# An intermediate of a two-stage transform, laid out in DRAM by the first stage's row

## The chip, the cores and the metric

The kernel runs on one core of a Trainium2 chip, in one launch. The metric is the device time of that launch in microseconds. Engines are named as in the profile: PE does matmuls, DVE and POOL element-wise work, ACT activations and copies, SP only issues DMAs (ACT issues some too).

## The reference: what is computed

A causal convolution of length 12480 in two batches of 128 channels, with a filter that a small network makes from position embeddings, and then two dense layers with 2048 hidden units each. Only the convolution is touched by the change.

```
h = (relu(pos_emb @ w1) @ w2) * exp(-0.01 * pos)      # the filter, 12480 x 128
u = x * v                                             # 2 x 12480 x 128
y = causal convolution of u with h along the sequence # in the reference by FFT of length 24960
a = x * y
b = relu(a @ moe_w_in) ** 2 @ moe_w_out
c = b @ moe2_w_in ;  out = (c * cos(c)) @ moe2_w_out
```

## The kernel before

The convolution is a transform by matmuls in two stages (12480 = 104 x 120), a product, and the way back. Stage 1 is a DFT over 104 rows (padded to 112) for each of the 120 columns. Stage 2 is a DFT over the columns for each of the 104 resulting rows, the product of signal and filter spectrum, and the inverse of stage 2. Stage 3 (not touched) does the inverse over 104 and the two dense layers; its inputs come from the intermediate `Ds` in DRAM.

Stage 1 goes in 30 chunks q of two column pairs i. For a chunk, `load` issues four DMAs on SP: positions `pt` (128 rows), `xt`, `vt` and the DFT table `et` (112 rows each), with five buffers each. `mlp1` makes the hidden layer of the filter network, `prep` runs up to five pairs ahead, multiplies x by v on POOL and scales the filter, and `pair` does eight matmuls `A` and the butterfly on ACT, DVE and POOL into `bt` (two buffers, 112 rows x 8 x 384). Each chunk's `bt` is stored to the intermediate `Bs` in DRAM by a DMA on ACT's queue, issued after the first pair of the next chunk. The order of the instructions on each engine is the order of the program. Meanwhile `decode` splits the weights of the dense layers in small steps on DVE, ACT and POOL; each step needs a load of raw weights on SP.

`Bs` is laid out by the second stage's row: [120 rows p, 2 halves c, 112 first-stage rows k, 384]. So a store writes, for each of 112 partitions, eight runs of 384 numbers (1.5 KB), and `load2` of stage 2, which takes four k for all p, reads two runs of 1536 numbers (6 KB) for each of 120 partitions.

Stage 2 goes in 26 groups g of four k. `spectrum` does the matmul `H` of the filter part of a group, `product` the matmuls `Z` of the signal part, `inverse` the way back, `butterfly` writes `dt`, which is stored to `Ds`. B2 has three buffers; `load2(g + 3)` is issued once group g is done with its own.

The end of stage 1 is written by hand. Group 0's B2 lies in a pool of its own, `B20`. With the first pair of the last chunk, SP issues the load of its rows 0 to 111; the rows 112 to 119 come straight from `bt` in SBUF, by `first`: four DMAs of 6 KB for each pair of the last two chunks, 16 in all. The last chunk is stored in two halves by `store1`. Groups 1 and 2 are loaded at the start of stage 2, after the second of these stores.

Of the kernel before, what the change touches and what calls it, by code (L numbers as in the profile page):

```python
# [22 lines left out]
NP = 112  # L23
# [11 lines left out]
WORDER = [0, 1, 2, 3, 4, 5, 6, 7, 8, 12, 9, 13, 10, 14, 11, 15]  # L35
LA = LDB = 5
WRATE = (3, 2, 1, 4)
WS = 54
# [10 lines left out]
def conv_moe(ctx, tc, t):  # L49
# [68 lines left out]

    c0 = ctx.enter_context(tc.tile_pool(name="c0", bufs=1))
    B20 = c0.tile([2 * HB, 2, G4, 384], F32, name="B2_0")  # L120

    def load2(B2, g, rows=slice(0, 2 * HB)):
        nc.sync.dma_start(out=B2[rows].rearrange("p c k e -> p c (k e)"),
                          in_=Bs[rows, :, G4 * g:G4 * (g + 1), :].rearrange("p c k e -> p c (k e)"))


    with ExitStack() as st:
        c1 = st.enter_context(tc.tile_pool(name="c1", bufs=1))
        ld1 = st.enter_context(tc.tile_pool(name="ld1", bufs=LDB))
        io = st.enter_context(tc.tile_pool(name="io1", bufs=2))  # L130
# [8 lines left out]
        ld = {}  # L139
        Bk = Bs.rearrange("p c k e -> k (p c) e")  # L140

        def load(q):
            pt = ld1.tile([128, CB, NP], F32, tag="pos", name="pt")
            xt = ld1.tile([NP, CB, 2, 256], F32, tag="xt", name="xt")
            vt = ld1.tile([NP, CB, 2, 256], F32, tag="vt", name="vt")
            et = ld1.tile([NP, CB, 2, NP], F32, tag="et", name="et")
            nc.sync.dma_start(out=pt, in_=t["posT"][q])
            nc.sync.dma_start(out=xt, in_=t["xl"][q])
            nc.sync.dma_start(out=vt, in_=t["vl"][q])
            nc.sync.dma_start(out=et, in_=t["E"][q])  # L150
            ld[q] = (pt, xt, vt, et)

# [23 lines left out]
        def pair(q, i):  # L176
            if i == 0:
                bt_t[q] = ld1.tile([NP, CB, 2, 2, 384], F32, tag="bt", name="bt", bufs=2)
            et, u, bt = ld[q][3], ut_t[q], bt_t[q]
# [22 lines left out]

        def store1(q, i):
            b = CB * q + i
            nc.scalar.dma_start(out=Bk[:, 4 * b:4 * b + 4, :], in_=bt_t[q][:, i].rearrange("k r c e -> k (r c) e"))

        def first(q, i):
            b = CB * q + i
            for c in range(2):
                for r in range(2):  # L210
                    p = 2 * b + r
                    nc.sync.dma_start(out=B20[p:p + 1, c].rearrange("b k e -> b (k e)"), in_=bt_t[q][0:G4, i, r, c, :])

        def store(q):
            nc.scalar.dma_start(out=Bk[:, 4 * CB * q:4 * CB * (q + 1), :],
                                in_=bt_t.pop(q).rearrange("k b r c e -> k (b r c) e"))

# [18 lines left out]
        for n, (q, i) in enumerate(seq):  # L236
# [5 lines left out]
            if i == 0 and q:  # L242
                store(q - 1)
            if (q, i) == (NCH - 1, 0):
                load2(B20, 0, slice(0, 2 * (HB - 2 * CB)))
            if q >= NCH - 2:
                first(q, i)
            if q == NCH - 1 and i == 1:
                for e in range(CB):
                    store1(q, e)  # L250
            if i == 1:
# [22 lines left out]
    with ExitStack() as st:  # L274
# [6 lines left out]
        decode(WG)  # L281
        NB = 3
        B2 = [B20] + [c2.tile([2 * HB, 2, G4, 384], F32, name=f"B2_{n}") for n in range(1, NB)]

        hs = {}

        def spectrum(g, c):
            H = psH.tile([128, G4, D], F32, tag="H", name="H")
            nc.tensor.matmul(H, Gt[:, c, :], B2[g % NB][:, c, :, 256:384], start=True, stop=True)
            hr = hk.tile([128, G4, D], F32, tag=f"hr{c}", name=f"hr{c}")  # L290
            hi = hk.tile([128, G4, D], F32, tag=f"hi{c}", name=f"hi{c}")
            nc.scalar.activation(hi[0:64], H[64:128], AF.Copy, scale=-1.0)  # L292
            nc.scalar.activation(hi[64:128], H[64:128], AF.Copy)  # L293
            if c == 0:
                for e in range(2):
                    nc.scalar.activation(hr[64 * e:64 * e + 64], H[0:64], AF.Copy)  # L296
            hs[g, c] = (hr, hi, H)
# [10 lines left out]
        def product(g, j, c):  # L308
            hr, hi, _ = hs[g, c]
            Z = psZ.tile([128, 2, 2, D], F32, tag="Z", name="Z")  # L310
            nc.tensor.matmul(Z, Gt[:, c, :], B2[g % NB][:, c, 2 * j:2 * j + 2, 0:256], start=True, stop=True)
            w = wk.tile([128, 2, 2, D], F32, tag="w", name="w")
# [58 lines left out]

        for n in range(1, NB):
            load2(B2[n], n)
        seq = [(g, j) for g in range(NG) for j in range(G4 // 2)]
# [8 lines left out]
        for n in range(len(seq) + 4):  # L383
# [16 lines left out]
            if n < len(seq) and seq[n][1] == 1 and seq[n][0] + NB < NG:  # L400
                load2(B2[seq[n][0] % NB], seq[n][0] + NB)

# [280 lines left out]
def host(inp):  # L683
# [6 lines left out]
    for s, d in (("x", "xl"), ("v", "vl")):  # L690
        a = inp[s].reshape(2, N1, 2, NCH, CB, D)
        out[d] = c(pad(a.transpose(3, 1, 4, 2, 0, 5), 1)).reshape(NCH, NP, CB, 2, 256)
    p = inp["pos_emb"].reshape(N1, 2, NCH, CB, 64)
    out["posT"] = c(pad(p.transpose(2, 1, 4, 3, 0), 4)).reshape(NCH, 128, CB, NP)
    out["w1"] = c(inp["w1"])
# [25 lines left out]
```

## Time and profile before

| | |
|---|---|
| median of three runs | 2890.15 us (2887.17 to 2894.08) |
| the profiled execution's own time | 2895.59 us |
| its span from first to last instruction | 2893.8 us |
| PE, DVE, ACT, POOL busy over the span | 96%, 84%, 86%, 49% |
| DMA moved | 214.99 MB, mean 74 GB/s |

Busy time is the time with an instruction running. An idle time of an engine is put down to what released it last. A DMA is seen twice: as an issue on the queue of an engine (SPq, ACTq), which is short, and as packets on the 16 DMA engines.

### The profile page before, as it was taken

How to read it: one execution, taken by the hardware profiler on the slowest of the kernel's cores; microseconds unless marked ns; L12 is line 12 of the kernel's file. 1: busy time of each engine (PE TensorE's matmuls, PEld its weight loads, DVE VectorE, ACT ScalarE, POOL GpSimd, SP SyncE). 2: the span in 40 equal slices, each digit the busy share in tenths (PEclk: the TensorE clock that was granted, in tenths of full speed). 3: DMA queues.
4: the chain of work that ended last, by engine and by line, in shares of the span. 5: the costliest groups of instructions: out<-in, count | busy, mean ns of one | idle time of the engine just before them, and what ended most of it. 6: DMA issues, size and time to landing. Idle time of an engine off the chain costs nothing.

```text
span 2893.8 us, 39390 instructions
## 1 busy us (share of the span) xinstructions
PE 2770.2 (96%) x11740; PEld 2117.5 (73%) x11740; DVE 2418.6 (84%) x4844; ACT 2488.1 (86%) x4464; POOL 1420.7 (49%) x1112
## 2 busy tenths in 40 slices
PE   6778699889999999999999999999999999999999
PEld 3444233378888888888888888888888888888887
DVE  4778688878888888888888888888888888888888
ACT  4455699869999999999999999999999999999998
POOL 4666578714444444444444444444444444444445
PEclk9889799989999999999999999999999999999999
DMA  9998888721010111101100101111110001010000
GB/s 283 290 303 268 218 256 260 205 77 29 16 33 24 31 28 30 30 27 31 27 31 16 31 27 31 27 31 30 27 30 27 26 21 31 27 31 27 19 8 9
DMA packets 111661, 214.99 MB, mean 74 GB/s; under 512 B 7344, under 2 KB 85224, under 8 KB 111448
## 3 DMA queue, kind: packets, MB, share of 16 engines
q1 hardware_dynamic: 83217, 170.80, 20.6%
q10 hardware_dynamic: 28231, 41.69, 4.3%
q8 instruction: 92, 1.51, 0.2%
q14 instruction: 121, 0.99, 0.1%
HBM read 132.72 MB, written 79.63 MB: 73 GB/s over the span
## 4 chain that ended last, share of the span: by engine, by line
PE 78%; ACT 8%; DMA 2%; issue 2%; DVE 2%; SPq 0%; POOL 0%; POOLq 0%; DVEq 0%; ACTq 0%
PE h L490 13%; PE h L492 12%; PE h L491 12%; PE y L506 12%; PE y L505 12%; PE y L504 12%; PE pc L456 3%; ACT w L314 2%; ACT w L313 2%; ACT hr L296 1%; ACT hi L292 1%; DMA B<-Bs 1%; ACT ds L343 1%; ACT hi L293 1%; PE A L184 1%
## 5 line engine op out<-in xcount | busy, mean ns | idle before, releaser
L595 POOL TENSOR_TENSOR gl<-g,gh 128x512 fp32r<-128x512 f32 (+2 forms) x800 | 1034.1, 1293 | 1258.3 <-ACT gh L586 764.3
L578 DVE TENSOR_TENSOR g<-h,c 128x512 f32<-128x512 f32 (+2 forms) x800 | 537.6, 672 | 246.3 <-ACT c L570 239.8
L490 PE MATMUL h<-zh,wh 128*128 128x512 f32 (+2 forms) x1600 | 643.3, 402 | 0.7 <-DVE zh L474 0.7
L555 ACT ACTIVATE k<-h,quarter 128x512 int32<-128x512 f32 (+2 forms) x800 | 541.0, 676 | 114.6 <-PE h L492 100.5
L506 PE MATMUL y<-gl,wh 128*128 128x512 f32 (+2 forms) x1600 | 625.2, 391 | 5.2 <-POOL gl L595 2.5
L492 PE MATMUL h<-zh,wl 128*128 128x512 f32 (+2 forms) x1600 | 624.1, 390 | 0.0
L504 PE MATMUL y<-gh,wl 128*128 128x512 f32 (+2 forms) x1600 | 623.4, 390 | 0.1
L491 PE MATMUL h<-zl,wh 128*128 128x512 f32 (+2 forms) x1600 | 623.4, 390 | 0.0
L505 PE MATMUL y<-gh,wh 128*128 128x512 f32 (+2 forms) x1600 | 622.7, 389 | 0.0
L570 ACT ACTIVATE c<-r,halfpi 128x512 f32<-128x512 f32 (+2 forms) x800 | 565.2, 706 | 2.6 <-DVE r L563 2.6
L529 ACT ACTIVATE r<-h 128x512 f32<-128x512 f32 (+2 forms) x800 | 471.8, 590 | 99.8 <-PE h L492 83.1
L549 DVE TENSOR_TENSOR gl<-g,gh 128x512 fp32r<-128x512 f32 (+2 forms) x800 | 535.8, 670 | 1.0
L563 DVE CUSTOM_DVE_ANT_0 r<-h,k 128x512 f32<-128x512 f32 (+2 forms) x800 | 534.0, 667 | 0.0
L535 ACT ACTIVATE g<-r 128x512 f32<-128x512 f32 (+2 forms) x800 | 492.5, 616 | 2.1 <-DVE gl L549 1.5
L542 DVE CAST gh<-g 128x512 fp32r<-128x512 f32 (+2 forms) x800 | 331.1, 414 | 41.7 <-ACT g L535 40.0
L506 PEld LDWEIGHTS y<-gl,wh 128*128 128x128 f32 x1600 | 301.8, 189 | 76.8 <-POOL gl L595 7.7
L504 PEld LDWEIGHTS y<-gh,wl 128*128 128x128 f32 x1600 | 302.2, 189 | 67.2 <-DVE zl L517 0.5
L492 PEld LDWEIGHTS h<-zh,wl 128*128 128x128 f32 x1600 | 302.6, 189 | 66.6
L505 PEld LDWEIGHTS y<-gh,wh 128*128 128x128 f32 x1600 | 302.1, 189 | 66.6
L490 PEld LDWEIGHTS h<-zh,wh 128*128 128x128 f32 x1600 | 303.2, 190 | 58.1 <-DVE zh L474 0.9
L491 PEld LDWEIGHTS h<-zl,wh 128*128 128x128 f32 x1600 | 302.9, 189 | 56.1
L586 ACT ACTIVATE gh<-g 128x512 fp32r<-128x512 f32 (+2 forms) x400 | 246.2, 615 | 0.1
(65 smaller groups left out, 2671.9 us busy)
## 6 DMA issues: line engine op xcount, KB each, us to landing
Bs<-bt ACTq DMA_DIRECT2D x29, 1344.0 KB
B<-Bs SPq DMA_DIRECT2D x25, 1440.0 KB
dt<-Ds SPq DMA_DIRECT2D x59, 416.0 KB
Ds<-dt SPq DMA_DIRECT2D x25, 960.0 KB
xt<-xl SPq DMA_DIRECT2D x30, 448.0 KB
vt<-vl SPq DMA_DIRECT2D x30, 448.0 KB
xt<-xT SPq DMA_DIRECT2D x60, 208.0 KB
out<-o SPq DMA_DIRECT2D x47, 256.0 KB
```

The source lines that it names most:

```text
L490: nc.tensor.matmul(h[:, :n], wh[:, f, :], zh[:, :n], start=True, stop=False)
L491: nc.tensor.matmul(h[:, :n], wh[:, f, :], zl[:, :n], start=False, stop=False)
L492: nc.tensor.matmul(h[:, :n], wl[:, f, :], zh[:, :n], start=False, stop=True)
L504: nc.tensor.matmul(y[:, :n], wl[:, f, :], gh[:, :n], start=a, stop=False)
L505: nc.tensor.matmul(y[:, :n], wh[:, f, :], gh[:, :n], start=False, stop=False)
L506: nc.tensor.matmul(y[:, :n], wh[:, f, :], gl[:, :n], start=False, stop=b)
L549: nc.vector.tensor_tensor(out=gl[:, :n], in0=g[:, :n], in1=gh[:, :n].bitcast(F32), op=ALU.subtract)
L555: nc.scalar.activation(k[:, :n], hp[2, u][:, :n], AF.Identity, scale=-1.0, bias=quarter)
L563: nc.vector._custom_dve(TENSOR_ADD_SAT, out=r[:, :n], in0=h[:, :n], in1=k[:, :n], s0=0.25, s1=-0.75)
L570: nc.scalar.activation(c[:, :n], r[:, :n], AF.Sin, bias=halfpi, scale=TWO_PI)
L578: nc.vector.tensor_tensor(out=g[:, :n], in0=h[:, :n], in1=c[:, :n], op=ALU.mult)
L595: nc.gpsimd.tensor_tensor(out=gl[:, :n], in0=g[:, :n], in1=gh[:, :n].bitcast(F32), op=ALU.subtract)
```

## The change

`Bs` becomes [112 k, 240 (p, c), 384]: by the first stage's row. A store now writes one run of 8 x 384 numbers (12 KB) for each of 112 partitions; `load2` reads, for each of 120 partitions, four runs of 768 numbers (3 KB). x, v and the table of a chunk stand side by side in DRAM (`xve`) and come in one DMA of 112 rows x 2496 numbers (10 KB); the positions keep theirs. Both land in one slot of 128 x 3072 numbers. Of the five slots three belong to a pool `ring` that outlives stage 1: they become the three B2 of stage 2. `bt` moves to the pool io.

The hand-written end changes. With the first pair of the last chunk (q = 29), after the store of chunk 28, SP issues `load2` for groups 0, 1 and 2 with rows 0 to 115. After the second pair, ACT's queue stores the first 16 rows (k = 0 to 15) of the last chunk, SP issues `load2` for the three groups with rows 116 to 119, and ACT's queue stores rows 16 to 111. `first`, `store1` and the loads at the start of stage 2 go. Matmuls of stage 2 read B2 with k outside and c inside.

```diff
--- before.py
+++ after.py
@@ -34,6 +34,8 @@
 OFF = 24
 WORDER = [0, 1, 2, 3, 4, 5, 6, 7, 8, 12, 9, 13, 10, 14, 11, 15]
 LA = LDB = 5
+NB = 3
+XVE, SLOT0, SLOT = 2048 + 4 * NP, 2048 + 6 * NP, 3072
 WRATE = (3, 2, 1, 4)
 WS = 54
 WG = 16
@@ -116,17 +118,24 @@
         for _ in range(n):
             next(steps, None)
 
-    c0 = ctx.enter_context(tc.tile_pool(name="c0", bufs=1))
-    B20 = c0.tile([2 * HB, 2, G4, 384], F32, name="B2_0")
-
-    def load2(B2, g, rows=slice(0, 2 * HB)):
-        nc.sync.dma_start(out=B2[rows].rearrange("p c k e -> p c (k e)"),
-                          in_=Bs[rows, :, G4 * g:G4 * (g + 1), :].rearrange("p c k e -> p c (k e)"))
+
+    conv_st = ExitStack()
+    ring = conv_st.enter_context(tc.tile_pool(name="ring", bufs=NB, side="right"))
+    Bg = Bs.rearrange("k (p c) e -> p k (c e)", c=2)
+    B2 = {}
+
+    def slot(name, pool=ring):
+        return pool.tile([128, SLOT], F32, tag="ld", name=name)
+
+    def load2(g, rows=slice(0, 2 * HB)):
+        if g not in B2:
+            B2[g] = slot("B2").rearrange("p (k c e) -> p k c e", k=G4, c=2)
+        nc.sync.dma_start(out=B2[g][rows].rearrange("p k c e -> p k (c e)"), in_=Bg[rows, G4 * g:G4 * (g + 1), :])
 
 
     with ExitStack() as st:
         c1 = st.enter_context(tc.tile_pool(name="c1", bufs=1))
-        ld1 = st.enter_context(tc.tile_pool(name="ld1", bufs=LDB))
+        ring1 = st.enter_context(tc.tile_pool(name="ring1", bufs=LDB - NB, side="right"))
         io = st.enter_context(tc.tile_pool(name="io1", bufs=2))
         wk = st.enter_context(tc.tile_pool(name="wk1", bufs=2))
         psA = st.enter_context(tc.tile_pool(name="psA", bufs=6, space=PSUM))
@@ -137,18 +146,15 @@
         win = c1.tile([NP, NCH, CB, 2], F32, name="win")
         tw = c1.tile([NP, 3], F32, name="tw")
         ld = {}
-        Bk = Bs.rearrange("p c k e -> k (p c) e")
 
         def load(q):
-            pt = ld1.tile([128, CB, NP], F32, tag="pos", name="pt")
-            xt = ld1.tile([NP, CB, 2, 256], F32, tag="xt", name="xt")
-            vt = ld1.tile([NP, CB, 2, 256], F32, tag="vt", name="vt")
-            et = ld1.tile([NP, CB, 2, NP], F32, tag="et", name="et")
-            nc.sync.dma_start(out=pt, in_=t["posT"][q])
-            nc.sync.dma_start(out=xt, in_=t["xl"][q])
-            nc.sync.dma_start(out=vt, in_=t["vl"][q])
-            nc.sync.dma_start(out=et, in_=t["E"][q])
-            ld[q] = (pt, xt, vt, et)
+            sl = slot("ld", ring if q % LDB < NB else ring1)
+            nc.sync.dma_start(out=sl[:, XVE:SLOT0], in_=t["posT"][q])
+            nc.sync.dma_start(out=sl[0:NP, 0:XVE], in_=t["xve"][q])
+            x, v = (sl[0:NP, 1024 * n:1024 * (n + 1)].rearrange("p (i a d) -> p i a d", i=CB, a=2) for n in range(2))
+            et = sl[0:NP, 2048:XVE].rearrange("p (i r k) -> p i r k", i=CB, r=2)
+            pt = sl[:, XVE:SLOT0].rearrange("p (i k) -> p i k", i=CB)
+            ld[q] = (pt, x, v, et)
 
         ut_t, hT_t = {}, {}
 
@@ -175,7 +181,7 @@
 
         def pair(q, i):
             if i == 0:
-                bt_t[q] = ld1.tile([NP, CB, 2, 2, 384], F32, tag="bt", name="bt", bufs=2)
+                bt_t[q] = io.tile([NP, CB, 2, 2, 384], F32, tag="bt", name="bt", bufs=2)
             et, u, bt = ld[q][3], ut_t[q], bt_t[q]
             A = {}
             for a in (1, 0):
@@ -200,20 +206,9 @@
             nc.vector.tensor_tensor(out=bt[:, i, 1, 0, :], in0=A[0, 1], in1=v[1], op=ALU.add)
             nc.gpsimd.tensor_tensor(out=bt[:, i, 1, 1, :], in0=e, in1=v[1], op=ALU.subtract)
 
-        def store1(q, i):
-            b = CB * q + i
-            nc.scalar.dma_start(out=Bk[:, 4 * b:4 * b + 4, :], in_=bt_t[q][:, i].rearrange("k r c e -> k (r c) e"))
-
-        def first(q, i):
-            b = CB * q + i
-            for c in range(2):
-                for r in range(2):
-                    p = 2 * b + r
-                    nc.sync.dma_start(out=B20[p:p + 1, c].rearrange("b k e -> b (k e)"), in_=bt_t[q][0:G4, i, r, c, :])
-
-        def store(q):
-            nc.scalar.dma_start(out=Bk[:, 4 * CB * q:4 * CB * (q + 1), :],
-                                in_=bt_t.pop(q).rearrange("k b r c e -> k (b r c) e"))
+        def store(q, rows=slice(0, NP)):
+            nc.scalar.dma_start(out=Bs[rows, 8 * q:8 * (q + 1), :].rearrange("k x e -> k (x e)"),
+                                in_=bt_t[q][rows].rearrange("k b r c e -> k (b r c e)"))
 
         nc.vector.memset(w1b, 0.0)
         nc.vector.memset(w2b, 0.0)
@@ -241,13 +236,16 @@
             upto("mlp", mlp1, (n + lead) // CB + 2 if n else 1, NCH)
             if i == 0 and q:
                 store(q - 1)
-            if (q, i) == (NCH - 1, 0):
-                load2(B20, 0, slice(0, 2 * (HB - 2 * CB)))
-            if q >= NCH - 2:
-                first(q, i)
-            if q == NCH - 1 and i == 1:
-                for e in range(CB):
-                    store1(q, e)
+            if q == NCH - 1:
+                if i == 0:
+                    for g in range(NB):
+                        load2(g, slice(0, 2 * CB * (NCH - 1)))
+                else:
+
+                    store(q, slice(0, 16))
+                    for g in range(NB):
+                        load2(g, slice(2 * CB * q, 2 * HB))
+                    store(q, slice(16, NP))
             if i == 1:
                 upto("load", load, q + LDB + 1, NCH)
             if 2 < n < WS:
@@ -279,14 +277,12 @@
         psH = st.enter_context(tc.tile_pool(name="psH", bufs=HB_, space=PSUM))
         psD = st.enter_context(tc.tile_pool(name="psD", bufs=DB, space=PSUM))
         decode(WG)
-        NB = 3
-        B2 = [B20] + [c2.tile([2 * HB, 2, G4, 384], F32, name=f"B2_{n}") for n in range(1, NB)]
 
         hs = {}
 
         def spectrum(g, c):
             H = psH.tile([128, G4, D], F32, tag="H", name="H")
-            nc.tensor.matmul(H, Gt[:, c, :], B2[g % NB][:, c, :, 256:384], start=True, stop=True)
+            nc.tensor.matmul(H, Gt[:, c, :], B2[g][0:2 * HB, :, c, 256:384], start=True, stop=True)
             hr = hk.tile([128, G4, D], F32, tag=f"hr{c}", name=f"hr{c}")
             hi = hk.tile([128, G4, D], F32, tag=f"hi{c}", name=f"hi{c}")
             nc.scalar.activation(hi[0:64], H[64:128], AF.Copy, scale=-1.0)
@@ -308,7 +304,7 @@
         def product(g, j, c):
             hr, hi, _ = hs[g, c]
             Z = psZ.tile([128, 2, 2, D], F32, tag="Z", name="Z")
-            nc.tensor.matmul(Z, Gt[:, c, :], B2[g % NB][:, c, 2 * j:2 * j + 2, 0:256], start=True, stop=True)
+            nc.tensor.matmul(Z, Gt[:, c, :], B2[g][0:2 * HB, 2 * j:2 * j + 2, c, 0:256], start=True, stop=True)
             w = wk.tile([128, 2, 2, D], F32, tag="w", name="w")
             nc.scalar.activation(w[0:64], Z[64:128], AF.Copy)
             nc.scalar.activation(w[64:128], Z[0:64], AF.Copy)
@@ -369,8 +365,6 @@
                     load_chunk(0, slice(0, N1 - G4))
                     load_aux(1)
 
-        for n in range(1, NB):
-            load2(B2[n], n)
         seq = [(g, j) for g in range(NG) for j in range(G4 // 2)]
         spectrum(0, 0)
         spectrum(0, 1)
@@ -398,7 +392,9 @@
             if n % 2 == 0:
                 decode(WRATE[2])
             if n < len(seq) and seq[n][1] == 1 and seq[n][0] + NB < NG:
-                load2(B2[seq[n][0] % NB], seq[n][0] + NB)
+                load2(seq[n][0] + NB)
+
+    conv_st.close()
 
 
     ck = ctx.enter_context(tc.tile_pool(name="ck", bufs=2))
@@ -689,9 +685,10 @@
     out["xT"] = c(a.transpose(2, 4, 3, 0, 1)).reshape(N2 // CI, D, CI, UT)
     for s, d in (("x", "xl"), ("v", "vl")):
         a = inp[s].reshape(2, N1, 2, NCH, CB, D)
-        out[d] = c(pad(a.transpose(3, 1, 4, 2, 0, 5), 1)).reshape(NCH, NP, CB, 2, 256)
+        out[d] = c(pad(a.transpose(3, 1, 4, 2, 0, 5), 1)).reshape(NCH, NP, 1024)
+    out["xve"] = np.concatenate([out.pop("xl"), out.pop("vl"), out.pop("E").reshape(NCH, NP, 4 * NP)], 2)
     p = inp["pos_emb"].reshape(N1, 2, NCH, CB, 64)
-    out["posT"] = c(pad(p.transpose(2, 1, 4, 3, 0), 4)).reshape(NCH, 128, CB, NP)
+    out["posT"] = c(pad(p.transpose(2, 1, 4, 3, 0), 4)).reshape(NCH, 128, CB * NP)
     out["w1"] = c(inp["w1"])
     out["w2"] = c(inp["w2"])
     for n in _W:
@@ -710,7 +707,7 @@
     arrays = host(inputs)
     t = {n: nc.dram_tensor(n, a.shape, mybir.dt.from_np(a.dtype), kind="ExternalInput").ap() for n, a in arrays.items()}
     t["out"] = nc.dram_tensor("out", (D, NT), F32, kind="ExternalOutput").ap()
-    t["Bs"] = nc.dram_tensor("Bs", (2 * HB, 2, NP, 384), F32).ap()
+    t["Bs"] = nc.dram_tensor("Bs", (NP, 4 * HB, 384), F32).ap()
     t["Ds"] = nc.dram_tensor("Ds", (2, 2 * HB, N1, 256), F32).ap()
     with tile.TileContext(nc) as tc:
         with tc.manual_schedule():
```

## Rows read from the trace of the kernel before

**Rows 1.** The page of the profiled execution: the span, the busy time of the engines, and three lines of the span cut into 40 equal slices of 72.3 us (busy share of PE and of the DMA engines in tenths, and what the latter moved).

```profile
span 2893.8 us, 39390 instructions
...
PE 2770.2 (96%) x11740; PEld 2117.5 (73%) x11740; DVE 2418.6 (84%) x4844; ACT 2488.1 (86%) x4464; POOL 1420.7 (49%) x1112
...
PE   6778699889999999999999999999999999999999
...
DMA  9998888721010111101100101111110001010000
GB/s 283 290 303 268 218 256 260 205 77 29 16 33 24 31 28 30 30 27 31 27 31 16 31 27 31 27 31 30 27 30 27 26 21 31 27 31 27 19 8 9
```

**Rows 2.** The table by stage: the start and end of each stretch, its length, the busy time of each engine with its instructions, PE's granted clock (as a share of 2.4 GHz), the mean busy share of the 16 DMA engines and what they moved. The stretches are stage 1 while it loads, stage 1 after its last load, the transition before and after the first matmul of stage 2, and stage 2.

```profile
37.70:248.90 211.20, 165.63 (x487) 94.12 (x486) 153.12 (x286) 105.01 (x252) 130.03 (x104) 0.88 0.95 303
248.90:290.80 41.90, 35.48 (x105) 19.46 (x103) 36.50 (x71) 23.05 (x51) 25.29 (x22) 0.91 0.70 227
290.80:304.20 13.40, 0.05 (x1) 0.08 (x1) 5.82 (x12) 1.26 (x2) 5.28 (x4) 0.50 0.77 214
304.20:319.90 15.70, 8.84 (x11) 3.31 (x12) 5.50 (x10) 5.91 (x10) 3.81 (x3) 0.61 0.84 210
319.90:571.00 251.10, 232.74 (x507) 90.94 (x505) 209.14 (x328) 241.88 (x409) 201.58 (x159) 0.99 0.83 239
```

**Rows 3.** The DMA issues of the whole span: destination and source, the queue that issues, how many, and KB each.

```profile
Bs<-bt ACTq DMA_DIRECT2D x29, 1344.0 KB
B<-Bs SPq DMA_DIRECT2D x25, 1440.0 KB
...
Ds<-dt SPq DMA_DIRECT2D x25, 960.0 KB
xt<-xl SPq DMA_DIRECT2D x30, 448.0 KB
vt<-vl SPq DMA_DIRECT2D x30, 448.0 KB
...
et<-E SPq DMA_DIRECT2D x30, 196.0 KB
...
pt<-posT SPq DMA_DIRECT2D x30, 112.0 KB
...
B<-bt SPq DMA_DIRECT2D x16, 6.0 KB
```

**Rows 4.** The waits of the engines in stage 1 while it loads (37.7 to 248.9 us): who waited for whom, us in total, times, longest.

```profile
DVE bt L198 <- DMA Bs<-bt: 27.5, 9, 5.1
```

**Rows 5.** The waits of SP's queue in the whole of stage 1 (0 to 292 us), same columns.

```profile
SPq L150 <- PE A L184: 123.9, 23, 12.2
```

**Rows 6.** The timeline of the transition (268 to 325 us): start, length, engine, line, operation, count, and in brackets the idle time before it and what ended it. SPq and ACTq are the queues that issue DMAs.

```profile
285.56 0.31 ACTq L215 DMA_DIRECT2D Bs<-bt  x1
...
286.87 0.56 DVE L198 TENSOR_TENSOR bt<-A,v 112x384 f32<-112x384 f32 x1 [0.95 <-DMA Bs<-bt]
...
290.25 0.54 DVE L200 TENSOR_TENSOR bt<-A,v 112x384 f32<-112x384 f32 x1
...
292.73 0.65 SPq L123 DMA_DIRECT2D B<-Bs  x1
...
293.48 11.11 SPq L212 DMA_DIRECT2D B<-bt  x8
...
304.15 3.82 PE L289 MATMUL H<-B,Gt 120*128 120x512 f32 x4 [16.21 <-DMA B<-Bs]
...
306.02 18.14 SPq L123 DMA_DIRECT2D B<-Bs  x3
306.23 0.59 ACT L292 ACTIVATE hi<-H 64x512 f32<-64x512 f32 x1 [7.35 <-PE H L289]
...
317.85 2.05 PE L289 MATMUL H<-B,Gt 120*128 120x512 f32 x2 [6.86 <-DMA B<-Bs]
...
319.94 0.59 ACT L292 ACTIVATE hi<-H 64x512 f32<-64x512 f32 x1 [7.65 <-PE H L289]
```

**Rows 7.** The DMA queues (q1 is SP's, q10 ACT's) in eight short windows in which one kind of transfer is all or nearly all there is: packets, MB, and the time that the packets took as a share of 16 engines' time in the window. In order: weights on 128 rows, 306.6 to 308 us (mostly 1 KB runs) and 308 to 309 (mostly 4 KB runs); stage 1's loads, 15 to 20; the first load of B on 112 rows, 298 to 300; a load of B on 120 rows, 312 to 317; stores of Bs, 258 to 261 and 267 to 268.5; the last stores of Ds, 584 to 585.

```profile
q1 hardware_dynamic: 492, 0.51, 103.4%
...
q1 hardware_dynamic: 136, 0.44, 107.5%
...
q1 hardware_dynamic: 560, 1.34, 104.8%
...
q1 hardware_dynamic: 76, 0.45, 106.6%
...
q1 hardware_dynamic: 180, 1.01, 95.1%
...
q10 hardware_dynamic: 596, 0.92, 99.2%
...
q10 hardware_dynamic: 344, 0.52, 101.6%
...
q1 hardware_dynamic: 90, 0.32, 88.4%
```

**Rows 8.** The timeline of SP's queue in stage 2 (345 to 565 us), two loads of B in a row of one group each.

```profile
459.04 0.84 SPq L123 DMA_DIRECT2D B<-Bs  x1
...
468.81 0.84 SPq L123 DMA_DIRECT2D B<-Bs  x1
```

## The prediction

> **What bounds the kernel now.** I read the page first, for its slices [rows 1]: the DMA engines are at 7 to 9 tenths in the first eight slices of 40 and at 2 or less after, while PE is full from slice 10 on. So the change, which touches only the first two stages, has to be priced there; the 2,320 us behind them are bound by PE and only move as a whole. The table by stage [rows 2] says what each part is bound by. Stage 1, while it still loads (37.7 to 248.9 us), holds the DMA engines at 0.95 with DVE at 73% and PE at 78%: it is bound by DMA. After its last load (to 290.8) the share falls to 0.70 and DVE is at 87%. From 290.8 to 319.9 lies the transition: PE works 8.9 us of 29. Then stage 2 runs with ACT busy 241.9 of 251.1 us, and no wait of an engine for a transfer is listed there; its loads follow each other every 9.77 us [rows 8], and that is ACT's time for a group.
>
> The chain in stage 1 runs through the store: DVE waited 27.5 us in nine places for a store to land before it could write a bt buffer again [rows 4], and SP's loads waited 123.9 us for PE to let go of the table [rows 5]. In the transition [rows 6], the last bt is written at 290.8, the big load of group 0 is issued at 292.73 when a store has landed, eight small `first` DMAs take SP until 304.6, H starts at 304.15, and ACT then idles another 7.65 us for group 1, whose load was issued at 306.02.
>
> **Prices of DMA.** From windows in which one kind of transfer is alone [rows 7] I take MB / (us x 16 x share), the rate of one engine while it is busy. Weights on 128 rows: 22.0 GB/s with 1 KB runs, 25.6 GB/s with mostly 4 KB runs. Stage 1's loads on 112 rows: 16.0. The load of B: 13.2 with 112 rows, 13.3 with 120. Stores of 1.5 KB runs: 19.3 and 21.3. Stores of Ds with 4 KB runs: 22.6.
>
> The same rows show how many engines take part. A transfer alone of 112 or 128 rows shows 103 to 108% (packets overlap a little), that of 120 rows 95.1%, that is 15.2 of 16. 112 and 128 split into 16 equal shares, 120 into 15 of 8 rows. My reading: a transfer goes to as many engines, up to 16, as share its rows equally. 116, the rows of the new first loads, is 4 x 29, so four engines would do all of it.
> The Trainium skill has this as a rule (DMA: Bandwidth & Descriptors, section "Why a DMA increments its semaphore by 16 and not by 1"): the largest number up to 16 that divides the outermost counts of both sides. By that rule 112 rows go to 16, 120 to 15, 116 and 4 rows to 4; the trace agrees for 112 and 120, and no row here shows four. It speaks against the change, and the sum below is the same with or without it.
>
> **The change, part by part.**
> *Store.* A chunk's store is 1344 KB [rows 3], 1.376 MB, now in 112 runs of 12 KB in place of 896 of 1.5 KB. At 20.3 GB/s (middle of the two rows) it costs 4.24 us of all 16 engines; at the 22.6 of the 4 KB runs 3.81, at the best rate of any row (25.6) 3.36. No row of a store gets slower with longer runs. So -0.43 us a chunk, between 0 and -0.88.
> *Loads.* The same 1204 KB a chunk [rows 3] in two DMAs, x, v and table as one run of 10 KB. SP's issue time is hidden behind its wait for PE, so it is worth nothing. The rate stays that of 112 rows, 16.0; if long runs on 112 rows bring it to the 13.2 of the 6 KB runs, a chunk's 1.233 MB cost 5.84 us in place of 4.82, +1.0. I take nothing, as the row nearest in place and in rows is this stage's own.
> *Shared slots.* x and v were free once POOL had multiplied them, the table once PE was done; now the whole slot waits for PE. SP issues in order and already stood at the table's load, so pt, x and v of the next chunk move back by up to one chunk of 9.6 us. They then have about two chunks until POOL needs them, against a load of 4.8 us beside a store of 4.2. Nothing, unless loads get slower, in which case PE and POOL wait next.
> Stage 1 together: 23 chunks x 0.43 x 0.95 = -9 us; bounds -20 and +23.
> *Transition.* The 16 `first` DMAs go, and with them SP's 11.11 us [rows 6]. In their place three loads of 116 rows, 1392 KB each by 120 rows' 1440 [rows 3], 4.28 MB in all, are issued where the old one was, at 292.7 (the store before must have landed, as now). On four engines that is 1.07 MB each. The slow rates of 13 to 16 belong to loads that run on 15 or 16 engines at once, some 200 to 260 GB/s in all; four engines ask for 100. So I take 24, inside the 22.0 to 25.6 of the undisturbed loads: 44.5 us. Bounds: 41.8 at 25.6, 80.4 at 13.3. The 96 rows of the last store put 74 KB on each engine, at 22.6 another 3.3 us. The three loads of the last four rows, again four engines, 37 KB each: 1.5 us, and they stand behind the 4.28 MB in the same queue, so that storing 16 rows first buys no early start. Issue and landing: 2.5 us, from the store of 285.56, which landed at 292.7 in 7.1 us where its 1.376 MB at 300 GB/s take 4.6. H then starts at 292.7 + 44.5 + 3.3 + 1.5 + 2.5 = 344.5 in place of 304.15: +40.4. All three groups are there by then, so the gap of 7.65 us falls away: +32.7, bounds +30 and +69.
> *Decoding* of weights waits for loads that now queue behind the 116 rows; its 9.4 us wait moves along with H and lies beside it. Nothing.
> *Stage 2.* B's load comes in 480 runs of 3 KB in place of 240 of 6 KB. Between the 1 KB and the 4 KB row a run costs some 8 ns beyond its bytes; 240 more over 15 engines are 0.13 us. The DMA share of 0.83 against 0.95 for a full queue leaves 1.2 us a group, and a load has two groups' time. Nothing; only beyond 1.2 us would DMA take over from ACT.
> Stage 3 keeps its work and its waits.
>
> **Sum.** The profiled execution took 2895.59 us: -9 + 33 gives 2919. It lies 5.4 above the median of the runs, 2890.15, so 2914.
>
> **The rivals.**
> *116 rows spread over 15 or 16 engines after all.* For it: every large transfer here is near 16. Against it: the 95.1% of the 120 rows. The place is the same three loads: 4.42 MB at 15.2 to 16 x 13.3 are 21 us, with 3.3 and 2.5 H starts at 319.5, +15.4, less 7.65 is +7.7. With -9 in stage 1 the kernel comes to 2889, no change. This is the case that can end on the other side: from 0.62 us saved a chunk (-13.5) it is faster by more than can be told, and at the bound of -20 it takes 2878.
> *Four engines at the slow rate.* 80.4 us in place of 44.5: 2950. For it: all loads into fewer than 128 rows are slow here. Against it: these are slow together, not each.
> *Stage 1 gets slower.* Loads at 13.2 or a lookahead too short by one chunk: half of the bound, +12 in place of -9, 2935. For it: SP's 123.9 us for PE [rows 5]; against it: two chunks remain.
> *The last four rows don't queue.* Then group 0 is there after 14.8 us, group 1 after 29.7, and ACT does up to two groups (19 us, say 17) under the rest: +16, 2897. Against it: one queue, few engines, issued last. The Trainium skill (same page, section "Queues, rings and completion order") says that each engine takes its transfers from a queue in order; by that rule this rival falls, and no row here shows it.
>
> **How the numbers follow.** Forecast 0.56, its own range 2898 to 2940 (stage 1 between -20 and 0, 22 to 25.6 GB/s and some disturbance); spread over all engines 0.22, split between no change (0.10) and faster (0.12); slow rate 0.08; stage 1 slower 0.08; no queueing 0.06, on the edge, half of it no change. A measurement can tell about 0.2%, 6 us, so slower is 0.56 + 0.08 + 0.08 + 0.03 = 0.75, same 0.10 + 0.03 = 0.13, faster 0.12. The range goes from 2880, which leaves the best of the spread case out, to 2945, short of the slow rate's 2950.
>
> **What would show it.** In the table by stage of the changed kernel: between the last bt and the first H some 50 us with a DMA share near 0.25 and about 100 GB/s, and PE waiting for B<-Bs once, not twice. In stage 1: a DMA share still above 0.9, stores' chunk intervals near 9.2 us, fewer waits of DVE for Bs<-bt. In stage 2: still 9.77 us a group and no wait for B. I am wrong if the transition shows a share near 0.95 (the split into equal shares falls), if H starts within 30 us of the load's issue, or if stage 1 moves by more than 20 us.

## The result, and the profile after

The changed kernel takes 2914.06 us (median of four runs, 2911.53 to 2914.99) against 2890.45 (four runs) for the kernel before: 1.0085 times as long, with a 95% interval of 1.0069 to 1.0102. The profiled execution took 2913.34 us with a span of 2911.5. Run once more later, the same kernel gave 1.0073 (1.0052 to 1.0095). One execution of all those below, the profiled one of the kernel by groups with 112 rows, was disturbed (3624.95 us at a granted clock of 0.70): it counts in no ratio, and no row of it is shown. The page, to be read against [rows 1]; a slice of 40 is now 72.8 us:

```profile
span 2911.5 us, 39267 instructions
...
PE   7885499979999999999999999999999999999999
...
DMA  9996499730110101010100111010100001010000
GB/s 301 327 328 222 122 256 259 222 97 25 30 30 27 31 27 30 16 41 16 33 28 27 30 27 30 27 31 16 42 28 23 27 25 31 27 31 27 19 8 9
```

The second and third slice went from 290 and 303 GB/s to 327 and 328, and slices 4 and 5 fell from 268 and 218 to 222 and 122, with PE at 5 and 4 tenths. The table by stage, with the columns and the order of stages of [rows 2] (stage 1 while it loads, stage 1 after its last load, the transition, stage 2):

```profile
38.90:243.10 204.20, 170.43 (x534) 95.44 (x533) 166.28 (x313) 113.81 (x275) 142.45 (x113) 0.96 1.02 330
243.10:271.20 28.10, 21.16 (x57) 10.90 (x55) 22.19 (x43) 12.99 (x27) 14.30 (x14) 0.88 0.59 205
271.20:329.20 58.00, 0.06 (x1) 0.09 (x1) 5.81 (x12) 1.26 (x2) 5.28 (x4) 0.52 0.38 116
329.20:590.00 260.80, 239.62 (x519) 93.89 (x520) 216.31 (x341) 247.83 (x420) 205.52 (x162) 0.99 0.82 228
```

Stage 1 is shorter, with a DMA share of 1.02 (over 1, as the packets' times overlap) where 0.95 stood. The transition has one matmul in 58 us. Stage 2 is as it was: from H to the last stores of Ds it takes 270.1 us, before 277.7 with the gap of 7.65 us in it [rows 6]. The timeline of the transition, to be read against [rows 6]:

```profile
271.27 0.78 ACTq L210 DMA_DIRECT2D Bs<-bt  x2
...
272.52 42.79 SPq L133 DMA_DIRECT2D B<-Bs  x6
...
315.41 0.41 SPq L81 DMA_DIRECT2D wr<-moe_w_out  x1
...
329.14 3.75 PE L285 MATMUL H<-B,Gt 120*128 120x512 f32 x4 [60.61 <-DMA B<-Bs]
...
331.56 0.43 DVE L96 TENSOR_SCALAR w_a<-wr 128x512 int32<-128x512 int32 x1 [51.75 <-DMA wr<-moe_w_out]
```

The first load of B is issued at 272.52 in place of 292.73, 20.2 us earlier. H starts 56.6 us after that issue in place of 11.4. That is +45.2; the gap of 7.65 us before group 1 [rows 6] is gone. Together -20.2 + 45.2 - 7.65 = +17.3, and the span of the profiled execution grew by 17.7. The DMA queues inside the hole (280 to 310 us; packets, MB, share of 16 engines' time):

```profile
q1 hardware_dynamic: 914, 2.79, 25.7%
```

A quarter of 16 engines is four: 2.79 MB in 30 us, 93 GB/s, 23 for each of the four. A load also reports its landing in parts, and the trace keeps them: each of the six loads here has four, the loads of 120 rows in stage 2 have 15.

### The profile page after: what moved, and what is told of

The parts are those of the page before. It is cut to its first block, busy times and chain, and to the rows that moved or that the text cites. A ratio compares the mean times of both kernels' runs of the same rounds, so it can differ in the third digit from the quotient of the medians.

```text
span 2911.5 us, 39267 instructions
## 1 busy us (share of the span) xinstructions
PE 2756.9 (95%) x11740; PEld 2108.9 (72%) x11740; DVE 2418.9 (83%) x4844; ACT 2486.7 (85%) x4464; POOL 1421.5 (49%) x1112
## 4 chain that ended last, share of the span: by engine, by line
PE 78%; ACT 8%; DMA 2%; DVE 2%; issue 2%; SPq 1%; POOL 0%; POOLq 0%; DVEq 0%; ACTq 0%
PE h L486 12%; PE h L488 12%; PE h L487 12%; PE y L502 12%; PE y L501 12%; PE y L500 12%; PE pc L452 4%; ACT w L310 2%; ACT w L309 2%; DMA Bs<-bt 1%; DMA B<-Bs 1%; ACT hr L292 1%; ACT hi L288 1%; ACT hi L289 1%; ACT ds L339 1%
```

## The experiments

Two questions were open. What makes the loss: by the forecast, that 116 rows go to four engines; by its rival, the order of the loads, with group 0 standing behind the others. And what gave stage 1 more than I forecast: long runs that save the engines' time, stores that land sooner so that bt comes free sooner, or the merged loads. Each expectation tells what it holds for which theory. A kernel's ratio is to the kernel before, timed on the same chip.

**112 rows first, 8 rows last.** The load's rows 0 to 111 and 112 to 119, nothing else.
```diff
-                        load2(g, slice(0, 2 * CB * (NCH - 1)))
+                        load2(g, slice(0, 112))
-                        load2(g, slice(2 * CB * q, 2 * HB))
+                        load2(g, slice(112, 2 * HB))
```


> The changed kernel with one number other: the three first loads of B take rows 0 to 111 in place of 0 to 115, and the loads behind the last store rows 112 to 119. Theory (116 rows run on four engines because they don't split into more equal shares): 112 rows split into 16, so the DMA share between the load's issue and the first H is near 1.0 and not 0.26, the way from issue to first H falls from 56.6 us to 27 to 32 us (4.13 MB at 211 GB/s are 19.6, the last store 3.3, the rest 4 to 9), and the kernel takes about 2887 us (2882 to 2893). Rival (the three loads are slow because of their 3 KB runs, the stores beside them or the order): the same volume and order stay, so 2914 us within 6.

Measured: 2879.72 us, ratio 0.9958 (0.9944 to 0.9973). Its timeline of the transition:

```profile
271.16 15.18 SPq L133 DMA_DIRECT2D B<-Bs  x6
...
300.54 3.75 PE L285 MATMUL H<-B,Gt 120*128 120x512 f32 x4 [28.22 <-DMA B<-Bs]
...
304.44 0.43 DVE L96 TENSOR_SCALAR w_a<-wr 128x512 int32<-128x512 int32 x1 [20.82 <-DMA wr<-moe_w_out]
```

Issue to H is 29.4 us in place of 56.6, as expected; the time lies below its range. Each of the three first loads now lands in 16 parts. Four rows fewer in the first load turn the loss into a gain: the row count is the cause.

**112, 104 and 100 rows** for groups 0, 1 and 2, one execution.
```diff
+                R = (112, 104, 100)
-                        load2(g, slice(0, 2 * CB * (NCH - 1)))
+                        load2(g, slice(0, R[g]))
-                        load2(g, slice(2 * CB * q, 2 * HB))
+                        load2(g, slice(R[g], 2 * HB))
```


> The changed kernel with first loads of 112 rows for group 0, 104 for group 1, 100 for group 2 (the rest of the rows behind the last store), to see how many engines each takes. Theory (as many engines, up to 16, as share the rows equally): shares of about 1.0, then 0.81 (13 engines) and 0.63 (10), the last clearest because nothing else runs beside it. Rival (nearly all engines for any large transfer, and 116 slow for another cause): near 1.0 throughout. Time about 2890 us (2882 to 2900) by the theory.

Measured: 2882.17 us. Four windows of the transition (columns as in the table by stage; the share is the last but one):

```profile
280.00:285.00 5.00, 0.00 (x0) 0.00 (x0) 0.00 (x0) 0.00 (x0) 1.57 (x2) 0.50 0.95 202
285.00:290.00 5.00, 0.00 (x0) 0.00 (x0) 0.00 (x0) 0.00 (x0) 0.00 (x0) 0.50 0.86 173
290.00:295.00 5.00, 0.00 (x0) 0.00 (x0) 0.00 (x0) 0.00 (x0) 0.00 (x0) 0.50 0.79 173
295.00:300.00 5.00, 1.85 (x3) 0.84 (x4) 0.00 (x0) 0.00 (x0) 0.00 (x0) 0.50 0.65 126
```

The share falls in steps. 104 = 13 x 8 and 100 = 10 x 10 would show 81% and 63% alone; the windows mix the groups, so the shares agree with the division but do not separate the three counts. The parts in which the loads land do: 16 for the 112 rows, 13 for the 104, 10 for the 100.

**By groups, 112 rows.** Group 0's first rows before the store, then its last rows, then group 1, group 2.
```diff
-                    for g in range(NB):
-                        load2(g, slice(0, 2 * CB * (NCH - 1)))
+                    load2(0, slice(0, 112))
...
-                        load2(g, slice(2 * CB * q, 2 * HB))
+                        if g:
+                            load2(g, slice(0, 112))
+                        load2(g, slice(112, 2 * HB))
```


> As before with rows 0 to 111, and the order changed: only group 0's load goes ahead of the last store, then group 0's last rows, then the loads of groups 1 and 2, each followed by its last rows. Theory (loads wait for each other in the order of their issue, and group 0's last rows stood behind all three): the first H starts 13 to 17 us after the first load's issue, the other groups land each about 7 us later and ACT, with 9.77 us a group, never waits for them; about 2871 us (2864 to 2879), faster than either kernel. Rival (the order of issue doesn't matter): as with rows 0 to 111 alone.

Measured: 2876.15 us (median of four), ratio 0.9945 (0.9929 to 0.9962), some 4 us better than the order before, which the two intervals do not tell apart; more was expected. The next kernel has the same order, and rows of that one are shown.

**By groups, 116 rows.** The same edit with 116 for 112.

> The changed kernel with its 116 rows, but in the order by groups: group 0's 116 rows, its last four, then group 1's, then group 2's. Theory (four engines, in order of issue): the first H about 23 us after the issue and not 56.6, then two more waits of PE for B<-Bs of some 5 us each; about 2898 us (2892 to 2904). Rival (the last four rows did not queue behind the 4.28 MB, or the four-row loads are slow by themselves): the first H stays beyond 50 us and the kernel at 2914 within 6.

Measured: 2911.89 us, ratio 1.0067 (1.0052 to 1.0083). The expectation failed. The timeline shows where:

```profile
273.09 42.77 SPq L133 DMA_DIRECT2D B<-Bs  x6
...
298.03 3.75 PE L285 MATMUL H<-B,Gt 120*128 120x512 f32 x4 [28.95 <-DMA B<-Bs]
...
313.21 2.05 PE L285 MATMUL H<-B,Gt 120*128 120x512 f32 x2 [8.43 <-DMA B<-Bs]
...
331.68 0.43 DVE L96 TENSOR_SCALAR w_a<-wr 128x512 int32<-128x512 int32 x1 [51.31 <-DMA wr<-moe_w_out]
...
337.65 1.92 PE L285 MATMUL H<-B,Gt 120*128 120x512 f32 x2
337.89 9.23 SPq L133 DMA_DIRECT2D B<-Bs  x2
```

H comes 25 us after the issue, as expected, 31 us earlier than in the changed kernel. Then DVE, which takes its instructions in order, stands at a decode step until 331.68. The raw weights for it are issued at 315.95, behind six loads on SP's queue. PE's next H, the second of group 1, follows at 337.65. The wait for weights that lay beside the wait for B, and was priced at nothing, is the next one in line.

**Weights loaded earlier.** The two kernels by groups, with raw weights fetched two steps ahead and three buffers for them.
```diff
-        raw = wt.tile([128, 4, 128, 2], I32, tag="wr", name="wr", bufs=2)
+        raw = wt.tile([128, 4, 128, 2], I32, tag="wr", name="wr", bufs=3)
-        n = WORDER.index(step) + 1
-        if n < 16:
-            raw_of(WORDER[n])
+        for n in (1, 2):
+            n += WORDER.index(step)
+            if n < 16 and WORDER[n] not in raws:
+                raw_of(WORDER[n])
```
With 112 rows:

> Rows 0 to 111 in the order by groups, and the raw weights loaded two steps ahead (three buffers) in place of one. It asks why the order by groups brought so little. Theory C (DVE works off its decoding steps before its first work of stage 2, and the weights for the second step were issued behind B's loads, so an early H waits on DVE): DVE's wait for wr before the first H goes, and the kernel takes about 2864 us (2857 to 2871). Rival (something else holds stage 2 back, such as loads of groups 1 and 2): 2876 us within 4.

With 116 rows:

> The same two steps ahead with the 116 rows in the order by groups. Theory C: the second group's work no longer waits for the weights behind 4.28 MB on four engines, and the kernel takes about 2898 us (2892 to 2904), as the order by groups alone was expected to. Rival: 2912 us within 4.

Measured with 112 rows: 2870.86 us, ratio 0.9931 (0.9916 to 0.9946). H starts 14.7 us after the issue (272.06 to 286.78) and DVE no longer waits for weights. With 116 rows: 2909.77 us, 1.0069 (1.0053 to 1.0086), again not what was expected. From its timeline:

```profile
280.08 42.52 SPq L134 DMA_DIRECT2D B<-Bs  x6
...
325.51 5.49 SPq L134 DMA_DIRECT2D B<-Bs  x1
...
344.29 2.05 PE L286 MATMUL H<-B,Gt 120*128 120x512 f32 x2 [15.38 <-DMA B<-Bs]
```

DVE's wait is gone, but PE waits at 344.29 for group 2, the last of the three that lie on four engines: its load left at 307.67, and two of its parts had landed by 332.6, the other two at 341.5 and 343.5 (its last rows at 344.15), beside the weights and group 3's load, which left at 325.51. In this execution B's first load also left 7.6 us later than in the changed kernel, which is not explained. With 116 rows some group was late in each of the three kernels tried. With 112 rows the same two edits are worth some 8 us (0.9958 to 0.9931).

**Three loads.** x, v and table in three DMAs again, else as changed.
```diff
-            nc.sync.dma_start(out=sl[0:NP, 0:XVE], in_=t["xve"][q])
+            for a, b in ((0, 1024), (1024, 2048), (2048, XVE)):
+                nc.sync.dma_start(out=sl[0:NP, a:b], in_=t["xve"][q][:, a:b])
```


> The changed kernel with x, v and table of a chunk in three DMAs again, into the same slot. It asks where stage 1's 20 us came from. Theory A (two DMAs of loads a chunk in place of four: SP no longer waits for earlier transfers to land before it may issue the next, and the queues stay full): the last chunk's store before the end is issued some 15 us later than at 266, the kernel takes about 2930 us (2922 to 2936). Theory B (the store's 12 KB runs): nothing changes, 2914 within 5.

Measured: 2916.1 us, ratio 1.0092 (1.0068 to 1.0117), no difference from the changed kernel that the intervals can tell; between 40 and 240 us a share of 1.02 and 328 GB/s, and B's first load leaves at 273.50, a microsecond later than in the changed kernel. Merging the loads is worth nothing in stage 1.

**The old layout of Bs**, else as changed: stores of 1.5 KB runs, loads of 6 KB runs.
```diff
-        nc.sync.dma_start(out=B2[g][rows].rearrange("p k c e -> p k (c e)"), in_=Bg[rows, G4 * g:G4 * (g + 1), :])
+        nc.sync.dma_start(out=B2[g][rows].rearrange("p c k e -> p c (k e)"),
+                          in_=Bs[rows, :, G4 * g:G4 * (g + 1), :].rearrange("p c k e -> p c (k e)"))
...
-    t["Bs"] = nc.dram_tensor("Bs", (NP, 4 * HB, 384), F32).ap()
+    t["Bs"] = nc.dram_tensor("Bs", (2 * HB, 2, NP, 384), F32).ap()
```


> The changed kernel with the intermediate laid out by the second stage's row again: stores in 1.5 KB runs, loads of B in 6 KB runs, all else as changed. Theory A (fewer DMAs): stage 1 keeps its 20 us, and 2914 us within 5. Theory B (long store runs, by their rate or by the share they get beside the loads): stage 1 loses 10 to 20 us, 2930 us (2922 to 2936). Stage 2's 9.77 us a group stay in both.

Measured: 2926.97 us, ratio 1.0123 (1.0105 to 1.0141), 13 us over the changed kernel; the share between 40 and 240 us is back at 0.94 with 298 GB/s. B's first load leaves at 298.27 here (in the slowest of the four executions) and at 285.85 in the control below, against 266.4 to 273.5 in the kernels above that have the new layout and fetch weights as before. So the layout is what made stage 1 faster. How long a store takes from issue to landing stands in the chain of waits of a stretch (start, us), for the stores that something waited for. Two of this kernel, then three of the changed one:

```profile
190.18 14.14 DMA Bs<-bt
...
227.79 17.16 DMA Bs<-bt
```

```profile
201.22 8.89 DMA Bs<-bt
...
217.08 10.75 DMA Bs<-bt
...
234.65 10.91 DMA Bs<-bt
```

These are the late ones. Over all stores issued between 40 and 240 us the time to the last part's landing is 6.3 to 17.2 us here, median 8.6, and 8.0 to 11.0 in the changed kernel, median 9.7. So the old layout's stores are not slower on the whole; some of them land late.

**A third bt buffer.** If stage 1 gains because bt comes free sooner, a third buffer should give the old layout the same, with no packet changed. Room for it is made by a shorter lookahead (LA 3, two buffers of ut); a control has the shorter lookahead alone.
```diff
-LA = LDB = 5
+LA, LDB = 3, 5
-                ut_t[q] = io.tile([NP, CB, 2, 384], F32, tag="ut", name="ut", bufs=3)
+                ut_t[q] = io.tile([NP, CB, 2, 384], F32, tag="ut", name="ut", bufs=2)
-                bt_t[q] = io.tile([NP, CB, 2, 2, 384], F32, tag="bt", name="bt", bufs=2)
+                bt_t[q] = io.tile([NP, CB, 2, 2, 384], F32, tag="bt", name="bt", bufs=3)
```
The control, old layout with two buffers:

> The control for the next run: intermediate by the second stage's row (stores in 1.5 KB runs), all else as changed, but stage 1 prepares three pairs ahead in place of five, with two ut buffers in place of three, which frees the room that a third bt buffer needs. Both theories: as with the old layout alone, about 2927 us, or a few us more where the shorter lookahead shows (2922 to 2935).

Old layout with three:

> The control with a third bt buffer. Theory B1 (the 1.5 KB runs cost stage 1 its time because a store takes 13 to 17 us to land beside the loads, and bt comes free late): the waits of DVE and POOL for Bs<-bt all but go, DMA's share in stage 1 rises from 0.94 to 1.0, and the kernel is 8 to 18 us faster than the control, about 2914 us. Theory B2 (the short runs cost the DMA engines' time itself): the third buffer only moves the wait, within 4 us of the control.

Measured: control 2927.82 us, ratio 1.0125 (1.0103 to 1.0146), as without the shorter lookahead. Three buffers: 2893.79 us (ten runs), ratio 1.0014 (1.0001 to 1.0027), which is 34 us less than the control and more than expected. Stage 1 between 40 and 240 us, control and three buffers, in the columns of the table by stage:

```profile
40.00:240.00 200.00, 158.21 (x468) 89.93 (x467) 156.11 (x280) 101.30 (x242) 124.46 (x101) 0.90 0.95 308
```

```profile
40.00:240.00 200.00, 170.32 (x544) 98.22 (x544) 177.01 (x327) 116.67 (x280) 145.14 (x118) 0.96 1.02 346
```

With 1.5 KB runs and three buffers DVE waits for no store in this stretch (18.7 us in the control), POOL 5.7 us (27.2), and stage 1 moves 346 GB/s, more than the changed kernel's 330. B's first load leaves at 255.42, and 54.6 us of four engines follow; that is why it only draws level with the kernel before.

**By groups, 112 rows, and a third bt buffer**, both edits from above in the changed kernel.

> Rows 0 to 111 in the order by groups, with the third bt buffer and the shorter lookahead. The new layout's stage 1 already has a DMA share of 1.02, so by B1 and B2 alike little is left: 2873 us (2867 to 2881), beside 2876 with two buffers. If waits for Bs<-bt (20 us on DVE) still are the bound there: 2862 us or less.

Measured: 2869.49 us, ratio 0.9925 (0.9904 to 0.9945), with the version above that fetches weights early the fastest of all runs. B leaves at 257.14 and H starts at 272.31, 32 us before that of the kernel before [rows 6]. DVE then waits 18.1 us for weights until 287.40, and some 10 us are lost again: from H to the last stores of Ds it takes 280.6 us, in the changed kernel 270.1. Early weights and three bt buffers together, and the old layout with 112 rows and three buffers, were not tried.

**The changed kernel again**, for the spread of its stages.

> The changed kernel again, unchanged, on the same chip as these runs: how much its stage 1 and its transition differ from one profile to another. 2914 us within 5; the last 16-row store issued at 271 us within 5, the first H 52 to 65 us after the first load of B is issued.

Measured: 2912.82 us. B's first load at 271.29, H at 328.63, 57.3 us: both stages repeat within about a microsecond. The spread of stage 1 is wider than these two show: with the rows mixed, and the same stage 1, that load left at 266.42.

## Why the prediction came out

**The time was right within a microsecond, in part by luck; two of its terms were off, with opposite signs.** Forecast: -9 for stage 1, +40.4 and -7.65 for the transition, in all +23.7. Measured: -20.2, and 45.2 - 7.65 = +37.5, in all +17.3. The rest is spread: the profiled execution of the kernel before lay 5.1 us above its median, that of the changed kernel 0.7 below, so between the medians the change cost 23.6. If that spread lies in stage 1, which no run shows, stage 1 gained some 14 us and not 20.

**Four engines: right, and shown.** The share is 25.7%, the loads land in four parts, and 112 rows undo it. The rival of 15 or 16 engines falls. The Trainium skill's rule (DMA: Bandwidth & Descriptors, "Why a DMA increments its semaphore by 16 and not by 1"), the largest number up to 16 that divides the outermost counts, now has its row for four as well, and for 13 and 10 in the kernel with mixed rows.

**Their rate: right.** 93 GB/s against the 96 taken (4 x 24); 4.28 MB take 46.0 us in place of 44.5. "Four engines at the slow rate" falls. One execution of the kernel with three loads showed a slower transfer, 67.6 us from issue to H, so the term has some spread of its own: there two of the four engines landed group 0's last rows by 323.9, the other two at 340.4 and 341.0.

**The rest of the transition: 4.8 us too small in all.** Issue to H is 56.6 where the terms add up to 51.8: 1.5 from the rate; the last store's packets hold the engines until about 277, 4.5 us after the issue where 3.3 were taken. The last 2 us go with unequal engines: the four parts of group 0's last rows landed at 323.2, 324.7, 327.8 and 329.1, and H waits for the last, where the sum took four equal ones. Why two engines are later is not shown.

**The last four rows queue: right.** In the changed kernel H started as group 0's four rows landed (329.05), about a microsecond before the last of the six loads (330.2), and with these rows placed behind group 0's own first load it started 25 us after the issue. Their load also left late, at 298.89, as SP was still held by the loads ahead of it. The gain that the rival promised for early groups did not come even so: in that order the time stayed at 2911.89.

**Decoding: right, under its cover.** "Nothing" holds while B is later. DVE's weights came at 331.56, 2.4 us after H; as soon as H was early, they set the next group.

**The store in stage 1: the failed step.** I priced the store's bytes, 20.3 against 22.6 GB/s an engine, and got -9. Measured was -20.2 between the profiled executions, at the bound of the term and past the 20 us that were to show it wrong. Alone on the engines the store's rate didn't rise. The ACT queue alone in the changed kernel, 255 to 258 us:

```profile
q10 hardware_dynamic: 79, 0.97, 99.0%
```

That is 0.97 MB / (3 us x 16 x 0.99) = 20.4 GB/s an engine with 12 KB runs, between the 19.3 and 21.3 of 1.5 KB runs [rows 7]. The gain came from the wait for a store's landing instead. In the 28 intervals between the first and the last full store a chunk took 9.20 us before and 8.46 after. The two queues between 40 and 240 us of the changed kernel, then of the old layout with three bt buffers:

```profile
q1 hardware_dynamic: 9663, 33.76, 62.9%
q10 hardware_dynamic: 2979, 32.06, 38.8%
```

```profile
q1 hardware_dynamic: 9770, 34.13, 53.1%
q10 hardware_dynamic: 23149, 34.94, 48.2%
```

For each busy engine the sum of both queues moved 20.2 GB/s in the first (65.82 MB / (200 us x 16 x 1.017)) and 21.3 in the second, where the store has 23149 packets in place of 2979; in the control it is 20.3, by its row above. So long runs saved no engine time. What they changed is the division between the queues: the loads' packets took 62.9% for 33.76 MB where they take 53.1% for 34.13 MB, the store's 38.8% for 32.06 MB where they take 48.2% for 34.94 MB. And fewer stores landed late. Of those issued between 40 and 240 us the latest took 11.0 us (12.4 in the kernel with 112 rows, which has the same stage 1), where it was 14.7 in the kernel before and 14.4 in the control; the medians, 9.7, 9.3 and 7.7, did not fall. DVE and POOL both write bt, so a late store holds both; their waits for one, beside [rows 4], first POOL's of the kernel before (37.7 to 248.9 us), then those of the changed kernel (38.9 to 243.1):

```profile
POOL bt L201 <- DMA Bs<-bt: 23.5, 8, 5.2
```

```profile
DVE bt L204 <- DMA Bs<-bt: 19.8, 13, 4.4
...
POOL bt L207 <- DMA Bs<-bt: 9.9, 8, 2.1
```

Together they fell from 51.0 to 29.7 us. I had read a share of 0.95 as a full queue; the 5% were engines idle while DVE and POOL stood at a bt buffer [rows 4], as the third buffer shows, which ended nearly all of that wait and brought the share from 0.95 to 1.02. The wait was on my page and I didn't price it. PE's mean granted clock between 40 and 240 us rose as well, from 0.87 to 0.96 of 2.4 GHz, but it did not set the length of stage 1: with 112 rows, and the same stage 1, it was 0.92, and B's first load left at 271.16.

Why some stores with short runs land late beside loads is not shown. The Trainium skill (same page, "Queues, rings and completion order") says that an engine alternates between queues a packet at a time, a packet being several descriptors; by that rule a store of short packets would get the smaller share beside long ones. With three bt buffers the stores of 1.5 KB runs took 12.4 us (median), those of 12 KB runs 10.55, which agrees with it but leaves other causes open.

**Merged loads, stage 2: right.** Three DMAs gave the same time. Stage 2's loads are still 9.77 us apart, and PE waited for B once:

```profile
PE H L285 <- DMA B<-Bs: 60.6, 1, 60.6
```

**Shared slots: right in price.** SP now waits 180.4 us for PE in stage 1 (25 times) where 123.9 stood [rows 5], and the DMA share still rose, so that wait cost nothing that shows.

## What to carry to other kernels

Choose the row count of a DMA's outer dimension as one would choose a tile: 116 in place of 112 rows cost some 30 us here (34 between the medians, 2914.06 and 2879.72, and 28 between the spans of the profiled executions), more than the rest of the change brought. When a share near 0.95 stands beside an engine that waits for a store's landing, price the landing and the buffer count, not the bytes: one more buffer moved stage 1 further than a new layout. And before an early start is priced, look for the wait that lies beside the one removed, and for the queue that the next load must leave by.

## What the hardware showed that was not expected

Loads that ran on few engines held the queue that issues them. Of the six loads of the changed kernel, issuing alone took 42.4 us on SP (of the merged row's 42.79), a single one up to 17.5; of the old layout's six, on four engines too, 31.3. The same loads with 112 and 8 rows took 5.2: the merged row's 15.18 holds two waits beside. A load of 120 rows took 0.82 to 0.93 in the kernel before, where the 18.14 of [rows 6] holds a wait as well, and 0.84 alone in stage 2 [rows 8]. So a slow transfer also delays the issue of unrelated loads, as the weights above.

Four engines did not run equally: in every kernel with 116 rows and the new layout two of the four parts of the last loads landed later than the other two, by some 4 us in the changed kernel and by 17 with three loads. And 12 KB runs wrote to DRAM at 20.4 GB/s an engine, no faster than 1.5 KB runs at 19.3 to 21.3; beside loads they cut the late landings, not the mean time.
